# Setup tables as planned steps, PSUM banks from the plan, and a given order for each engine up to the third up step

## The chip, the core and the metric

The kernel runs on one core of a Trainium2 chip. The metric is the device time of one execution in microseconds (us). Five engines work side by side, each through its own instructions in order: TensorE (PE, with its weight loads as PEld), VectorE (DVE), ScalarE (ACT), GpSimd (POOL) and SyncE (SP). SP and POOL also issue the DMA transfers of this kernel; an engine that waits at one instruction holds up all that stands behind it on the same engine.

## What is computed

The reference is an RWKV-style linear attention followed by an MLP mixer. There are 4 batches, 8 heads, 768 tokens and 48 channels a head (8 x 48 = 384 = `d_model`).

```python
for t in range(S):                                    # attention, for every batch and head
    cur = einsum('bhd,bhe->bhde', u * k[t], v[t])
    y[t] = einsum('bhd,bhde->bhe', r[t], state + cur)
    state = w * state + einsum('bhd,bhe->bhde', k[t], v[t])
x = y as [batch, token, 384]
h = relu(x^T @ w_tok1) @ w_tok2                       # mixes tokens: 768 -> 256 -> 768
u = x + h^T
out = u + relu(u @ w_ch1) @ w_ch2                     # mixes channels: 384 -> 1536 -> 384
```

## The kernel before

**Tiling.** The sequence of a batch is cut into 6 chunks of 128 tokens; one chunk of one batch is a *unit*, 24 in all (unit u belongs to batch u // 6). For a unit, k and r are multiplied by tables of powers of w, so that the recurrence becomes matrix products: inside the chunk a masked 128 x 128 product for each head, across chunks a state S.

**The steps of a unit, by the names of the plan.** `kp` and `rp` multiply the loaded k and r by the tables `wn` and `wp` into the tile `kpr` (on DVE or POOL). `trk` and `trr` transpose the two halves of `kpr` on PE into `tr_ps`; `rkk`/`rkr` (or one `rk`) copy the result to SBUF on ACT. `at` makes the scores on PE (`at_ps0`, `at_ps1`), and `AT0`, `AT1` mask them on DVE; where a unit is listed in `raw`, ACT first copies the scores to bf16 and DVE masks the copy. `pr` and `pg` give the term with u, `vb` casts v on ACT, `yd` multiplies it in, `kv` and `S` make the next state, `yS` and `y` the output in PSUM, and `x` adds up the unit's result on DVE.

**The mixer of a batch.** `hid` (w_tok1, 2 matmuls for each of 6 units, tiles `wtok`, `h_ps`), `hr` (its relu into `h1r`), `bk`/`ub`/`ux` (w_tok2), `us` and `tu`/`uT` (sum and transpose), then 2 x 12 *up steps* `z` (w_ch1, 3 matmuls of 384 columns each, tile `z_ps`) with their relus `zr`, and the *down steps* `h` (w_ch2, also named `wch`) with `os` and the store. Up and down steps of a batch are interleaved on PE with the attention units of the next one.

**What sets the order.** Function `graph` lists all steps with their predecessors, the engines they can run on and a time for each; class `Plan` then runs a list scheduler over them (`run`): at each moment the step of lowest `rank` that is ready gets a free engine. The instructions are issued in the order of the planned start, engine by engine, so the plan fixes each engine's order for good; its times do not bind the chip. The plan also treats transfers as steps: loads are issued by SP (`i:k6`, `i:r6`, ...; k, r and v of 192 KB each a unit), the seven weight transfers by POOL (`i:w0` to `i:w6`: 0 is w_tok1, 1 is w_tok2, 2, 6 and 4 are parts of w_ch1, 3 and 5 the halves of w_ch2). In the plan a transfer is one step on one resource "DMA", which takes one transfer at a time.

**Lines that matter here.** Loads of units 0 to 5 are issued at once at the start, in the order of `FIRST`. The load of k of unit 6 is held back until unit 5's output is made, and all later loads stand behind it on SP:

```python
    hold={6: ('y', 5), 21: ('us', '2_2')},
    wafter={0: 'x:r4', 1: 'x:r4', 2: 'rp5', 6: 'rp5', 4: 'kp5', 3: 'rp5', 5: 'rp5'},
```

The tables are set up outside the plan's view: the step `lnw` takes two logarithms on ACT and then, in the same step, three products on DVE (`wr`, the tile `wp`); the plan knows only the ACT part. In the units 13 to 15 the step `vb` also issues one more exponential on ACT (`wp_as_read`, tiles `wp<-lnw`), which the plan does not count. Four PSUM banks form a ring (pool `psM`) for transposes, up and down steps and others, and the framework hands them out. All engine instructions go through one helper, so the profile gives them one line (L515, in the changed kernel L579), and tiles tell them apart.

Of the kernel before, what the change touches and what calls it, by code (L numbers as in the profile page):

```python
# [23 lines left out]
T = 128  # L24
# [11 lines left out]
class Step:  # L36
    def __init__(self, name, ways, after, take, give, rank, emit):
        self.name, self.ways, self.take, self.give, self.rank, self.emit = name, ways, take, give, rank, emit
        self.after = [a for a in after if a is not None]
        self.then, self.left, self.ready = [], len(self.after), 0.0  # L40
        self.engine = self.start = self.end = self.seen = self.sends = None
        for a in self.after:
            a.then.append(self)


class Plan:
# [3 lines left out]
    def __init__(self, banks, busy_until, in_flight, relax_from=0.0):  # L50
        self.relax_from = relax_from
        self.steps, self.banks, self.busy_until, self.in_flight, self.used = [], banks, busy_until, in_flight, []
# [20 lines left out]
    def run(self):  # L73
# [4 lines left out]
        todo, times = len(self.steps), [0.0]  # L78
        while todo:
# [4 lines left out]
            while again:  # L84
                again = False
                for s in sorted(open_, key=lambda s: (s.rank, s.ready)):
# [8 lines left out]
                    way = min(s.ways, key=lambda w: max(now, free.get(w[0], 0.0)) + w[2] + (w[4] if len(w) > 4 else 0.0))  # L95
                    eng, busy, seen = way[:3]
                    shares = len(way) > 3 and way[3]
                    if free.get(eng, 0.0) > now:
                        continue
                    if shares and port["DVE" if eng == "POOL" else "POOL"] > now:  # L100
                        heapq.heappush(times, max(port.values()))
                        continue
                    s.engine, s.start, s.end, s.seen = eng, now, now + busy, now + seen
                    free[eng] = s.end
# [5 lines left out]
                    if s.take:  # L110
                        i = banks.index(min(banks))
                        banks[i], held[s.name] = float("inf"), i
                        self.used.append([now, float("inf"), s.name])
# [16 lines left out]
    def fill(self, since, until, least, margin, each, emit):  # L130

        mine = sorted((s for s in self.steps if s.engine == "PE"), key=lambda s: s.start)
        for a, b in zip(mine, mine[1:]):
# [4 lines left out]
            taken = sum(1 for x in self.used if x[0] < b.start and x[1] > a.end)  # L138
            n = int((b.start - a.end - margin) / each)
            if b.start - a.end >= least and taken < self.banks and n > 0:  # L140
                s = self.add(f"fill{a.name}", [("PE", n * each, n * each)], emit=emit(n))
                s.engine, s.start, s.end, s.seen = "PE", a.end, a.end + n * each, a.end + n * each
# [3 lines left out]
def products_in_turn(steps, apart):  # L146


    both = [s for s in steps if s.engine in ("DVE", "POOL") and s.name.rstrip("0123456789") in ("kp", "rp", "ku", "rku", "yd", "wGm")]
    dve = [s for s in steps if s.engine == "DVE"]  # L150
    behind, d = {}, None
    for s in both:
        if s.engine == "DVE":
            d = s if len(s.after) and s.name[:2] != "yd" or s.ways[0][0] == "POOL" else d
        elif d is not None and s.start - d.end < apart:
# [13 lines left out]
def graph(do, cfg):  # L169

    p = Plan(4, cfg.get("busy_until", dict(ACT=3.9, DVE=3.6, POOL=5.0, PE=5.4)), cfg.get("in_flight", 8), cfg.get("relax_from", 0.0))
# [10 lines left out]
    lnw = p.add("lnw", [("ACT", 0.49, 0.6)], rank=-100, emit=do("lnw"))  # L182
    tables, wps = {}, {}
    tables[0] = setup = p.add("wn0", [("ACT", 0.52, 0.65)], [lnw], rank=-99, emit=do("wn", 0))
    wps[0] = p.add("wp0", [("ACT", 0.52, 0.65)], [lnw], rank=-98, emit=do("wp", 0))
    for g in (1, 2):
        tables[g] = p.add(f"wn{g}", [("ACT", 0.52, 0.65)], [lnw], rank=g - 0.6, emit=do("wn", g))
        wps[g] = p.add(f"wp{g}", [("ACT", 0.52, 0.65)], [lnw], rank=g - 0.5, emit=do("wp", g))

    wu = p.add("wu", [("PE", 0.4, 0.6)], rank=-1, emit=do("wu"))  # L190
    uw = p.add("uw", [("DVE", 0.65, 0.8)], [wu], rank=0.05, emit=do("uw"))
# [4 lines left out]
    for n, (kind, i) in enumerate(cfg["transfers"]):  # L196
# [3 lines left out]
        elif kind != "w":  # L200
            for nm in cfg.get("lorder", "krv") if kind == "u" else kind:
                s = p.add(f"i:{nm}{i}", [("SP", cfg.get("sp", 0.65), 0.65)], fetched[-1:], rank=-1000 + n, emit=do("load", nm, i))
                fetched.append(s)
                gates[nm, i] = s
                loads[nm, i] = p.transfer(f"x:{nm}{i}", s, cfg.get("xload", {}).get(i, 1.01), cfg.get("xload", {}).get(i, 1.01) + 1.09 + cfg.get("slack", {}).get(f"{nm}{i}", 0.0), 0.0)
# [13 lines left out]
    for u in range(NU):  # L219
# [22 lines left out]
        else:  # L242
            trk = p.add(f"trk{u}", [("PE", 0.235 * f, 0.235 * f + 0.2)], [kp], take=True, rank=r, emit=do("trk", u))
            trr = p.add(f"trr{u}", [("PE", 0.235 * f, 0.235 * f + 0.2)], [rp, trk], rank=r - 0.5, emit=do("trr", u))
            if u == 0:
                p.wait(wu, [trr])
# [22 lines left out]
        a0 = p.add(f"AT0_{u}", [("DVE", 0.597, 0.75)], [atq[0]], rank=r, emit=do("AT", u, 0))  # L269
        if u in cfg.get("raw", ()):  # L270
            raw = p.add(f"raw{u}", [("ACT", 0.5, 0.65)], [at], rank=r, emit=do("raw", u))
            a1 = p.add(f"AT1_{u}", [("DVE", 0.33, 0.48, True)], [raw], rank=r, emit=do("ATr", u))
            at_free = [a0, raw]
        else:
            a1 = p.add(f"AT1_{u}", [("DVE", 0.597, 0.75)], [atq[1]], rank=r, emit=do("AT", u, 1))
            at_free = [a0, a1]
# [139 lines left out]
CFG = dict(apart=2.0,   # L416
    transfers=[("u", u) for u in range(0, 6)]
# [20 lines left out]
    slack={'v5': 3.0},  # L438
# [5 lines left out]
    cold=(1.8, 1.8, 1.8, 1.3),  # L444
    xload={6: 0.33},
    wtime=(3.0, 2.6, 1.55, 5.2, 3.1, 3.9, 1.55),
    raw=(0, 1, 5, 8, 11),
# [13 lines left out]
    warm=(2, 4),  # L461
# [6 lines left out]
def kernel(  # L468
# [32 lines left out]
    psM = ctx.enter_context(tc.tile_pool(name="psM", bufs=4, space=bass.MemoryType.PSUM))  # L501
# [41 lines left out]
    idle_ps = psM.tile([128, 512], f32, name="idle_ps", tag="m")  # L543
    w_ps = psM.tile([128, dm + 2 * D], f32, name="w_ps", tag="m")
# [6 lines left out]
    pe.matmul(w_ps[:, 0:dm], ones, row, start=True, stop=True, skip_group_check=True)  # L551
# [66 lines left out]
    def lnw_(eng):  # L618
        act.activation(lnw, w_ps[:, 0:dm], Ln)
        act.activation(lnr.rearrange("p q d -> p (q d)"), w_ps[:, dm:], Ln)  # L620
        shape = [128, 2, R, D]
        for g in range(G):
            dve.tensor_mul(wr[:, g], lnr.unsqueeze(2).to_broadcast(shape), iota_r[:, g].unsqueeze(1).unsqueeze(3).to_broadcast(shape))
# [11 lines left out]
    def wu(eng):  # L635
        M0["wu"] = psM.tile([128, 2, HP], f32, name="wu_ps", tag="m")
# [9 lines left out]
    def ubc(eng):  # L646
# [14 lines left out]
             ("k", 4, 0), ("r", 4, 0), ("v", 4, 0), ("r", 4, 1), ("r", 5, 0), ("k", 5, 0), ("r", 5, 1), ("v", 5, 0))  # L661
# [83 lines left out]
    def tr(j, i):  # L745
        if j == 0:
            L[i]["tr"] = psM.tile([128, 2, HP, T], bf16, name="tr_ps", tag="m")
# [51 lines left out]
    def raw(eng, i):  # L799
        L[i]["raw"] = apool.tile([128, HP, T], bf16, name="raw", bufs=2)  # L800
        act.copy(L[i]["raw"], L[i]["at"][1])

    def ATr(eng, i):
        L[i]["AT"][1] = apool.tile([128, HP, T], bf16, name="AT1", bufs=LEAD)
        dve.tensor_mul(L[i]["AT"][1], L[i]["raw"], mask_b.unsqueeze(1).to_broadcast([128, HP, T]))
# [11 lines left out]
    def pg(eng, i):  # L817
        own = i in CFG.get("ydp", ())
        to = psM.tile([128, H], f32, name="g_ps", tag="m") if own else kvs[1][:, i % G]
# [74 lines left out]
    def hid(eng, b, c):  # L894
        if c == 0:
            M[b]["h1"] = [psM.tile([128, dm], f32, name="h1_ps", tag="m") for _ in range(2)]
# [16 lines left out]
    def bk(eng, b, c):  # L913
        M[b]["bk", c] = psM.tile([128, dm], f32, name="hT_ps", tag="m")
# [12 lines left out]
    def tu(eng, b, c):  # L927
        M[b]["t", c] = psM.tile([128, 3, 128], bf16, name="t_ps", tag="m")
# [10 lines left out]
    def ux(eng, b, sg, m):  # L939
        if m < 2:  # L940
            M[b]["ut", sg, m] = psA.tile([128, HP, T], f32, name=f"at_ps{m}", tag=f"at{m}").rearrange("p a t -> p (a t)")[:, 0:dm]
        else:
            M[b]["ut", sg, m] = psM.tile([128, dm], f32, name="ut_ps", tag="m")
# [18 lines left out]
    def z(eng, b, sg, j):  # L962
        if (b, sg) not in Z:
            Z[b, sg] = zpool.tile([128, NJ, dm], bf16, name="zr")
        M[b]["z", sg, j] = psM.tile([128, dm], f32, name="z_ps", tag="m")
# [7 lines left out]
    def h(eng, b, c, q, part, parts):  # L973
        sg, si = divmod(c, 3)
        cols = ts(part, dm // parts)
        if q == 0:
            M[b]["h", c, part] = psM.tile([128, dm // parts], f32, name="h2_ps", tag="m")
# [81 lines left out]
```

## Time and profile before

| what | value |
|---|---|
| runs | 165.55, 165.68, 166.1 us; median 165.68 us |
| profiled execution | span 164.0 us from the first to the last instruction |
| median of the runs less that span | 1.68 us |
| PE busy | 156.6 us (95% of the span), 1466 matmuls |
| DVE, ACT, POOL busy | 109.2, 88.5 and 67.1 us |
| chain that ended last | PE 85%, DVE 5%, ACT 5%, issue 2% |
| DMA | 26.26 MB, mean 160 GB/s |

A span row gives, for each engine, its busy time in a stretch and its number of instructions; a timeline row gives the start in us, the length, the engine, the operation and its tiles, and in brackets how long the engine had been idle and what ended it. "q0" is the queue of the transfers that POOL issues, "q1" that of SP's. The granted clock of PE stands at 1.00 in all rows.

### The profile page before, as it was taken

How to read it: one execution, taken by the hardware profiler on the slowest of the kernel's cores; microseconds unless marked ns; L12 is line 12 of the kernel's file. 1: busy time of each engine (PE TensorE's matmuls, PEld its weight loads, DVE VectorE, ACT ScalarE, POOL GpSimd, SP SyncE). 2: the span in 40 equal slices, each digit the busy share in tenths (PEclk: the TensorE clock that was granted, in tenths of full speed). 3: DMA queues.
4: the chain of work that ended last, by engine and by line, in shares of the span. 5: the costliest groups of instructions: out<-in, count | busy, mean ns of one | idle time of the engine just before them, and what ended most of it. 6: DMA issues, size and time to landing. Idle time of an engine off the chain costs nothing.

```text
span 164.0 us, 3852 instructions
## 1 busy us (share of the span) xinstructions
PE 156.6 (95%) x1466; PEld 100.9 (62%) x1466; DVE 109.2 (67%) x225; ACT 88.5 (54%) x194; POOL 67.1 (41%) x83
## 2 busy tenths in 40 slices
PE   6798999999999999899999999999999999999992
PEld 3277865566677666566566565666656655666562
DVE  6679897602289889899899899977876582012021
ACT  3898662595488466789706450077253502914900
POOL 8748893000037848566875856204750000000000
DMA  4999999999798997999999972999990028012012
GB/s 92 221 223 207 173 154 173 192 194 232 153 231 233 190 213 220 196 238 180 217 231 133 263 135 67 203 231 194 194 240 4 0 53 216 19 52 96 0 48 96
DMA packets 87307, 26.26 MB, mean 160 GB/s; under 512 B 76665, under 2 KB 87290, under 8 KB 87290
## 3 DMA queue, kind: packets, MB, share of 16 engines
q1 hardware_dynamic: 83392, 22.88, 65.1%
q0 software_dynamic: 3888, 3.15, 13.1%
q8 instruction: 11, 0.18, 0.4%
q14 instruction: 6, 0.05, 0.2%
q10 hardware_dynamic: 10, 0.00, 0.0%
HBM read 20.65 MB, written 4.72 MB: 155 GB/s over the span
## 4 chain that ended last, share of the span: by engine, by line
PE 85%; DVE 5%; ACT 5%; issue 2%; POOL 1%; DVEq 0%; ACTq 0%
PE h_ps L515 33%; PE z_ps L515 29%; PE y_ps L515 5%; PE at_ps L515 5%; PE tr_ps L515 4%; PE hT_ps L515 3%; PE kv_ps L515 3%; ACT rk L515 2%; DVE AT L515 2%; DVE x_b L515 1%; PE w_ps L515 1%; DVE yd L515 1%; POOL kpr L515 1%; ACT wp L515 1%; ACT raw L515 1%
## 5 line engine op out<-in xcount | busy, mean ns | idle before, releaser
L515 ACT ACTIVATE zr<-z_ps 128x384 bf16<-128x384 f32 x94 | 45.4, 492 | 44.2 <-PE z_ps L515 44.1
L515 PE MATMUL z_ps<-uT,wch 128*128 128x384 bf16 x288 | 52.5, 326 | 0.2
L515 PE MATMUL h_ps<-wch,zr 128*128 128x384 bf16 (+1 forms) x300 | 52.5, 320 | 0.0
L515 PEld LDWEIGHTS <-zr 128*128 128x128 bf16 x300 | 27.9, 98 | 15.5 <-issue 0.2
L515 PEld LDWEIGHTS <-wch 128*128 128x128 bf16 x288 | 26.7, 98 | 16.1 <-issue 0.4
L515 POOL TENSOR_TENSOR yd<-vb,adg 128x384 f32<-128x384 bf16 x18 | 15.5, 859 | 42.2 <-ACT adg L515 25.1
L515 DVE TENSOR_TENSOR AT<-at_ps,mask 128x512 bf16<-128x512 f32 x43 | 27.9, 683 | 0.6 <-PE at_ps L515 0.5
L515 DVE TENSOR_TENSOR osb<-u_sb,h_ps 128x384 f32<-128x384 bf16 (+1 forms) x22 | 11.7, 532 | 23.5 <-PE h_ps L515 23.4
L515 POOL TENSOR_TENSOR kpr<-ld_r,wp 128x384 bf16<-128x384 f32 x16 | 17.0, 1064 | 5.3 <-DVE yd L515 2.2
L515 ACT COPY rk<-tr_ps 128x512 bf16<-128x512 bf16 x28 | 15.5, 589 | 5.5 <-PE tr_ps L515 5.1
L515 PEld LDWEIGHTS <-kpr 128*128 128x128 bf16 x192 | 13.6, 108 | 6.1 <-POOL kpr L515 2.6
L515 DVE TENSOR_TENSOR x_b<-y_ps,yd 128x384 bf16<-128x384 f32 x24 | 13.3, 552 | 5.8 <-PE y_ps L515 5.5
L515 POOL TENSOR_TENSOR kpr<-ld_k,wn 128x384 bf16<-128x384 f32 x15 | 15.5, 1031 | 2.1 <-PE z_ps L515 1.1
L515 PEld LDWEIGHTS <-rk 48*128 48x128 bf16 (+1 forms) x272 | 11.1, 100 | 6.4 <-issue 2.8
L515 PE MATMUL tr_ps<-ident,kpr 128*128 128x128 bf16 x112 | 12.3, 247 | 2.0 <-ACT rk L515 1.0
L515 ACT CAST vb<-ld_v 128x384 bf16<-128x384 f32 x24 | 12.3, 511 | 3.5 <-DMA ld_v<-in_v_dram 3.5
L515 DVE TENSOR_TENSOR u_sb<-x_b,hT_ps 128x384 bf16<-128x384 bf16 x21 | 10.4, 546 | 1.1 <-PE hT_ps L515 1.1
L515 PEld LDWEIGHTS <-wtok 128*128 128x128 bf16 x90 | 8.0, 98 | 4.8 <-issue 0.6
L515 PEld LDWEIGHTS <-AT 128*128 128x128 bf16 x192 | 8.6, 99 | 3.6 <-DVE AT L515 0.7
L515 PE MATMUL at_ps<-rk 48*128 48x128 bf16 x192 | 10.4, 233 | 0.4 <-ACT rk L515 0.4
L515 DVE TENSOR_TENSOR kpr<-ld_k,wn 128x384 bf16<-128x384 f32 x9 | 5.9, 658 | 7.0 <-DMA ld_k<-in_k_dram 7.0
L515 PE MATMUL h_ps<-x_b,wtok 128*128 128x384 bf16 x48 | 10.2, 326 | 0.1
(91 smaller groups left out, 154.2 us busy)
## 6 DMA issues: line engine op xcount, KB each, us to landing
ld_k<-in_k_dram SPq DMA_DIRECT2D x24, 192.0 KB, 3.6
ld_v<-in_v_dram SPq DMA_DIRECT2D x24, 192.0 KB, 3.7
out_dram<-osb SPq DMA_DIRECT2D x23, 192.0 KB, 2.5
ld_r<-in_r_dram SPq DMA_DIRECT2D x28, 96.0 KB, 3.2
ld_r<-in_r_dram SPq DMA_DIRECT2D x10, 192.0 KB, 3.8
wch<-in_moe_w_ch_dram POOLq DMA_DIRECT2D x3, 576.0 KB, 12.6
wtok<-in_moe_w_tok_dram POOLq DMA_DIRECT2D x2, 384.0 KB, 5.1
wch<-in_moe_w_ch_dram POOLq DMA_DIRECT2D x2, 288.0 KB, 5.6
```

Source lines behind the costliest of these rows:

```text
L515: ins = tc.keep_in_program_order(f(*args, **kw))
```

## The change

**Setup as steps.** The logarithm of w is taken in two halves (`ln0`, `ln1`), the one for r in `lnr`; the three products `wr0` to `wr2` become steps that may run on DVE or POOL. The plan gets times at which the four small inputs of the setup are there.

**Banks.** `Plan.run` notes the ring bank that it gives each step, and the kernel asks for just that bank (pool `psM` with four tags and one buffer each).

**A given order.** `CFG["order"]` lists, for PE, ACT, DVE and POOL, every step up to the third up step in a fixed order (the step sits at the front of its engine's list or it waits). `lands` gives a landing time for each of the 18 first loads, `half_clock` a time until which PE's steps are counted 1.85 times as long (in place of `cold`, factors for the first units). The first loads change places: the second half of r of unit 4 goes ahead of v of unit 4. `raw` moves from units 0, 1 and 5 (one half each) to unit 4 (one half) and unit 5 (both). The dummy matmuls at the start go from 2 + 4 to 2 + 3. The rest of the steps is placed by the list scheduler as before, from the state in which the given order leaves it.

```diff
+                    if s.name in self.place:
+                        if front(self.place[s.name]) != s.name:
+                            continue
+                        ways = [w for w in s.ways if w[0] == self.place[s.name]]
+                    else:
+                        ways = [w for w in s.ways if w[0] not in self.order or front(w[0]) is None]
...
+                    if eng == "PE" and now < self.half_clock:
+                        busy, seen = busy * 1.85, busy * 1.85 + seen - busy
...
-    lnw = p.add("lnw", [("ACT", 0.49, 0.6)], rank=-100, emit=do("lnw"))
+    lns = [p.add(f"ln{h}", [("ACT", 0.23, 0.40)], [pre["w" + "AB"[h]]], rank=-100 + 0.1 * h, emit=do("ln", h)) for h in range(2)]
+        wrs[g] = p.add(f"wr{g}", [("DVE", 0.467, 0.62, True), ("POOL", 0.955, 1.06, True)], [lnr], rank=-98 if g == 0 else g - 0.9, emit=do("wr", g))
...
+                if (nm, i) in cfg.get("lands", {}):
+                    gates[nm, i] = s
+                    loads[nm, i] = p.add(f"x:{nm}{i}", [("-", 0.0, cfg["lands"][nm, i])], rank=-5000)
+                    continue
...
+        POOL=(
+            "kp1 kp2 wGm kp3 rp3 kp4 rp4 i:w0 rp5 i:w1 i:w2"
+        ).split(),
...
-    cold=(1.8, 1.8, 1.8, 1.3),
+    half_clock=19.0,
-    wtime=(3.0, 2.6, 1.55, 5.2, 3.1, 3.9, 1.55),
-    raw=(0, 1, 5, 8, 11),
+    wtime=(2.4, 1.95, 1.6, 5.2, 3.1, 3.9, 1.55),
+    raw=((4, 1), (5, 0), (5, 1), (8, 1), (11, 1)),
...
-    psM = ctx.enter_context(tc.tile_pool(name="psM", bufs=4, space=bass.MemoryType.PSUM))
+    psM = ctx.enter_context(tc.tile_pool(name="psM", bufs=1, space=bass.MemoryType.PSUM))
+    def bank(shape, dtype, name, which=None):
+        return psM.tile(shape, dtype, name=name, tag=f"m{now[-1].bank if which is None else which}")
...
-             ("k", 4, 0), ("r", 4, 0), ("v", 4, 0), ("r", 4, 1), ("r", 5, 0), ("k", 5, 0), ("r", 5, 1), ("v", 5, 0))
+             ("k", 4, 0), ("r", 4, 0), ("r", 4, 1), ("r", 5, 0), ("k", 5, 0), ("r", 5, 1), ("v", 4, 0), ("v", 5, 0))
```

**What it moves on POOL.** The place is the issue of the weights. In the kernel before, POOL's order around it reads (`kpr_130<-ld_r` is `rp` of unit 5, `wtok_160` w_tok2, `wch_161` w_ch1 and `wch_162` w_ch2):

```order
L515 DMA wtok_160<-in_moe_w_tok_dram 128x2x768
L515 TENSOR_TENSOR kpr_130<-ld_k,wn 128x8x48
L515 TENSOR_TENSOR kpr_130<-ld_r,wp 128x2x4x48
L515 DMA wch_161<-in_moe_w_ch_dram 128x3x384 x2
L515 DMA wch_161<-in_moe_w_ch_dram 128x3x768
L515 DMA wch_162<-in_moe_w_ch_dram 128x6x384 x2
L515 TENSOR_TENSOR yd<-vb,adg 128x384
```

The same place in the changed kernel, where `kpr_132<-ld_k` is `kp` of unit 6:

```order
L579 DMA wtok_159<-in_moe_w_tok_dram 128x6x256
L579 TENSOR_TENSOR kpr_130<-ld_r,wp 128x2x4x48
L579 DMA wtok_160<-in_moe_w_tok_dram 128x2x768
L579 DMA wch_161<-in_moe_w_ch_dram 128x3x384 x2
L579 DMA wch_161<-in_moe_w_ch_dram 128x3x768
L579 TENSOR_TENSOR kpr_132<-ld_k,wn 128x8x48
L579 DMA wch_162<-in_moe_w_ch_dram 128x6x384 x2
L579 TENSOR_TENSOR yd<-vb,adg 128x384
```

The `kp` of unit 6, on DVE before, now stands on POOL between the parts of w_ch1 and the two halves of w_ch2; `kp` of unit 5 went to DVE.

**What it moves on PE.** The place is the end of the third up step (`z_ps`, three matmuls). Before, the fourth up step follows at once, and unit 6's first transposes come some 75 matmuls later, between two down steps (`h_ps`). In the changed kernel:

```order
L579 MATMUL z_ps<-uT,wch_161 128x384
L579 LDWEIGHTS wch_161
L579 MATMUL z_ps<-uT,wch_161 128x384
L579 LDWEIGHTS kpr_132
L579 MATMUL tr_ps<-ident,kpr_132 128x128
L579 LDWEIGHTS kpr_132
L579 MATMUL tr_ps<-ident,kpr_132 128x128
L579 LDWEIGHTS kpr_132
L579 MATMUL tr_ps<-ident,kpr_132 128x128
L579 LDWEIGHTS kpr_132
L579 MATMUL tr_ps<-ident,kpr_132 128x128
L579 LDWEIGHTS wch_161
```

The four transposes of unit 6's k stand directly behind the third up step, ahead of the fourth.

**What it moves on ACT.** The place is the relu of the token mixer of batch 1 (`h1r<-h_ps`, two of 384 columns). Before:

```order
L515 COPY rk<-tr_ps 128x512 x2
L515 ACTIVATE h1r<-h_ps 128x384 x2
L515 COPY adg<-kv_ps 128x8
L515 ACTIVATE wp<-lnw,iota 128x384
L515 CAST vb<-ld_v 128x384
L515 COPY rk<-tr_ps 128x512 x2
```

In the changed kernel:

```order
L579 COPY rk<-tr_ps 128x512 x2
L579 COPY adg<-kv_ps 128x8
L579 ACTIVATE wp<-lnw,iota 128x384
L579 CAST vb<-ld_v 128x384
L579 ACTIVATE h1r<-h_ps 128x384 x2
L579 COPY rk<-tr_ps 128x512 x2
```

The exponential and the cast of unit 13 went ahead of the two relus, and on PE the `kv` matmuls of unit 13, which read that cast, went ahead of the `hT_ps` matmuls that read the relus.

158 lines of the change are left out of this document (102 added, 56 removed), and 3 rows, old and new, of the table PE.

## The prediction

> **What bounds the kernel now.** I first read the busy time by stretches; the columns are PE, PEld, DVE, ACT and POOL busy (instructions), granted clock, DMA share and GB/s.
>
> ```profile
> 10.00:19.00 9.00, 8.20 (x106) 6.89 (x102) 8.49 (x20) 7.49 (x19) 5.83 (x7) 1.00 0.91 201
> 19.00:24.20 5.20, 4.96 (x85) 3.43 (x81) 4.96 (x10) 3.09 (x8) 5.18 (x7) 1.00 1.26 168
> 30.10:67.00 36.90, 36.78 (x411) 24.73 (x409) 23.44 (x48) 24.78 (x56) 13.99 (x15) 1.00 0.99 207
> 67.00:73.30 6.30, 5.55 (x71) 3.91 (x69) 5.93 (x13) 5.00 (x13) 4.02 (x5) 1.00 1.05 220
> 73.30:136.00 62.70, 62.70 (x563) 38.99 (x563) 51.78 (x97) 27.99 (x61) 28.08 (x29) 1.00 0.80 158
> ```
>
> From 30.1 us on, PE is idle for 0.12 us in 36.9, then loses 0.75 us around 70, and nothing up to 136. So whatever moves the third up step moves the end by as much, in either direction, and any wait put into PE's order after 30 us is paid in full. Before 27 us the chain of waits runs over DVE instead:
>
> ```profile
> 19.80 1.27 DVE AT L515 x2
> ...
> 26.55 0.57 DVE x_b L515
> 27.16 0.48 PE h_ps L515 x2
> ...
> 31.82 0.17 PE t_ps L515 x3
> 31.99 0.65 PE z_ps L515 x4
> ```
>
> Unit 5's result (`x`) ends at 27.1; three matmuls of 0.163 us behind 31.99 end the third up step; ends of matmuls are modelled, and I count 32.4. Those 5.3 us hold the same mixer steps in both kernels, so the gain at the front is what `x` of unit 5 gains.
>
> **Part 1, the front.** These rows show its start, and the products and masks of the first 26 us on DVE by kind:
>
> ```profile
> 4.33 0.49 ACT L515 ACTIVATE lnw<-w_ps 128x384 f32<-128x384 f32 x1 [1.41 <-PE w_ps L515]
> 5.61 1.27 POOL L515 TENSOR_TENSOR kpr<-ld_k,wn 128x384 bf16<-128x384 f32 x1 [0.99 <-POOL bm L515]
> 10.29 0.42 DVE L515 TENSOR_TENSOR pr<-tr_ps,rk 128x512 bf16<-128x512 bf16 x1
> ...
> L515 DVE TENSOR_TENSOR AT<-at_ps,mask 128x512 bf16<-128x512 f32 x9 | 5.9, 683 | 0.0
> L515 DVE TENSOR_TENSOR x_b<-y_ps,yd 128x384 bf16<-128x384 f32 x6 | 3.3, 551 | 1.0 <-PE y_ps L515 0.7 <-DVE pr L515 0.2
> L515 DVE TENSOR_TENSOR yd<-vb,g_ps 128x384 f32<-128x384 bf16 x6 | 3.3, 545 | 0.0
> L515 DVE TENSOR_TENSOR wp<-lnr,iota_r 128x384 f32<-128x384 f32 x3 | 2.3, 821 | 1.3 <-ACT lnr L515 1.3
> L515 DVE TENSOR_TENSOR kpr<-ld_k,wn 128x384 bf16<-128x384 f32 x1 | 0.5, 548 | 0.0
> ```
>
> The logarithm waited for all of `w_ps`; in halves I let it start some 0.7 us earlier, which puts the first k product at 4.9 on DVE (0.55) in place of 5.61 on POOL (1.27). From there DVE has 42 instructions up to `x` of unit 5, against 33 from 10.29 before: the same 9 full masks, 3 short ones, 6 `pr`, 6 `yd`, 6 `x`, but five k and r products instead of one, the three table products and the small ones for u. With the durations above (0.42 for `pr` and the short mask, 0.55 for `yd` and the tables when POOL is quiet) they add up to 22.3 us against 18.1. Before, 18.1 took 27.1 - 10.3 = 16.8 us, since one instruction starts before the last has ended; in that ratio 22.3 take 20.7, to 25.6, a gain of 1.5. With no wait left (two masks of 0.683 in 1.27 overlap by about 0.08 each) they take 18.9, to 23.8, a gain of 3.3. Some of the waits do go: POOL's `rp` of unit 4 waited for its load until 18.37, and its second half is now issued one place earlier. I take **-1.8**, nearer the ratio, and keep -0.8 to -2.8. The third up step then ends at 32.4 - 1.8 = 30.6. The banks of the ring cost nothing here: PE's 0.12 us idle up to 67 leaves no wait for a bank to remove.
>
> **Part 2, unit 6 behind the third up step.** PE's next instructions now are four transposes that read the k product of unit 6, on POOL, which waits for its load, which SP holds until unit 5's `y`. Before:
>
> ```profile
> 18.37 0.99 POOL L515 TENSOR_TENSOR kpr<-ld_r,wp 128x384 bf16<-128x384 f32 x1 [0.48 <-DMA ld_r<-in_r_dram]
> 20.12 1.02 POOL L515 TENSOR_TENSOR kpr<-ld_k,wn 128x384 bf16<-128x384 f32 x1
> 22.03 4.02 POOL L515 DMA_DIRECT2D wch<-in_moe_w_ch_dram x5
> 26.42 0.37 SPq L515 DMA_DIRECT2D ld_k<-in_k_dram  x1
> 37.50 0.56 DVE L515 TENSOR_TENSOR kpr<-ld_k,wn 128x384 bf16<-128x384 f32 x1 [5.11 <-DMA ld_k<-in_k_dram]
> 43.54 0.61 PE L515 MATMUL tr_ps<-ident,kpr 128*128 128x128 bf16 x8
> ```
>
> Issued at 26.42, that load was used at 37.50, 11.1 us later, and nobody noticed, since its transposes stood at 43.5. It was slow because the weights were on the way. What each queue moved (packets, MB, share) from 0 to 30.0 us for POOL's, then from 26.4 to 30.0, then from 30.0 to 35.5:
>
> ```profile
> q0 software_dynamic: 2170, 1.76, 42.6%
> ...
> q0 software_dynamic: 671, 0.69, 117.8%
> ...
> q0 software_dynamic: 998, 0.85, 94.8%
> q1 hardware_dynamic: 918, 0.18, 28.8%
> ```
>
> No byte of SP's queue moved in the first 3.6 us, then 0.033 MB/us beside 0.155 of the weights. In the changed kernel the load is issued 1.8 earlier, at 24.6. Ahead of it on POOL's queue stand w_tok1, w_tok2 and w_ch1, 1,920 KB or 1.97 MB, but not w_ch2. By 30.0 POOL's queue had moved 1.76 MB of these before; the first three now start some 0.3 to 0.8 us later and w_ch1 1 us earlier, so I leave its end at about 30.8. The load moves nothing until 28.2, 2.6 x 0.033 = 0.09 MB until 30.8, and the other 0.11 MB at some 0.2 MB/us until 31.4; with the 0.4 to 1 us that a landing takes beyond that, it is there at **32.0**. The product on POOL (1.02) ends at 33.0, the transposes start at 33.05, and PE has stood since 30.6: **+2.5**. Behind the transposes wait all up steps, and behind them ACT's and DVE's relus.
>
> For the bounds and the next part, the median times to landing and the first down step:
>
> ```profile
> ld_k<-in_k_dram SPq DMA_DIRECT2D x24, 192.0 KB, 3.6
> wtok<-in_moe_w_tok_dram POOLq DMA_DIRECT2D x2, 384.0 KB, 5.1
> 38.65 0.33 PE L515 MATMUL h_ps<-wch,zr 128*128 128x384 bf16 x1
> ```
>
> The median landing of a k load is 3.6 us, which gives 28.2 and a product at 29.2, no stall; the 11.1 us of before give 35.7 and transposes at 36.7, a stall of 6.1.
>
> **Part 3, w_ch2.** Its halves were the last two of the five issued from 22.03, at about 24.4 and 25.2; now they stand on POOL behind the product, at 33.0 and 33.8. A transfer of 384 KB landed in 5.1; 576 KB need 1 us more, 39.1, and 40 to 41 beside SP's loads. PE reaches its first down step 14 up steps of 0.49 behind the transposes (33.3), at 40.1; before it was at 38.65. The second half is needed 3.4 us after the first and takes 3 to 4 more. Between 0 and 2.0; I take **+0.4**.
>
> **Part 4, ACT in the mixer of batch 1.**
>
> ```profile
> 65.94 0.50 PE L515 MATMUL h_ps<-x_b,wtok 128*128 128x384 bf16 x2
> 66.31 0.87 ACT L515 ACTIVATE h1r<-h_ps 128x384 bf16<-128x384 f32 x2 [1.20 <-PE h_ps L515]
> 67.31 1.29 PE L515 MATMUL hT_ps<-h1r,wtok 128*128 128x384 bf16 x6
> 67.75 0.62 ACT L515 ACTIVATE wp<-lnw,iota 128x384 f32<-128x384 f32 x1
> 68.27 0.50 ACT L515 CAST vb<-ld_v 128x384 bf16<-128x384 f32 x1
> 68.82 0.33 PE L515 MATMUL kv_ps<-vb,kpr 128*128 128x96 bf16 x4 [0.22 <-ACT vb L515]
> 69.79 0.40 PE L515 MATMUL at_ps<-rk 48*128 48x128 bf16 x8 [0.45 <-ACT rk L515]
> ```
>
> The relus ended 1.2 us behind the last `h_ps`, hidden by down steps and transposes; the exponential and the cast came after, beside the six `hT_ps` matmuls. Now those two (0.52 + 0.40 = 0.92 from start to start) come first, `kv` waits for them, and `hT_ps` for the relus behind them. 0.92, plus some 0.65 of the relus uncovered since a down step no longer stands there, less the 0.67 that PE waited here before: **+0.9**; 0 if the last unit's scores hold PE longer, 2.0 if the transposes behind it wait too.
>
> **Sum.** 164.0 - 1.8 + 2.5 + 0.4 + 0.9 = 166.0 us for the span. The runs' median lies 1.68 above the profiled span (165.68), so **167.7 us**.
>
> **The rule that speaks against Part 2.** The Trainium skill ("DMA: Bandwidth & Descriptors", Queues, rings and completion order) says that each DMA engine goes round-robin between the queues for which it has work. By that, unit 6's load would move from the start, which the first 3.6 us of the row above contradict. It is the second rival.
>
> **The rivals.** (a) *The load is as quick as a lone one*, 3.6 us: no stall, w_ch2 in time, 164.0 - 1.8 + 0.9 = 163.1, so 164.8, faster. It decides where the load lands before 29.5. Only the dip of DMA traffic around 24 to 25 us before speaks for it, and w_ch1 now is issued into that dip. (b) *The load shares from about 1 us after its issue*: 0.033 x 5.2 = 0.17 MB by 30.8, landed at 31.0 at the latest, perhaps 30.6; product at 31.6, stall 1.1, w_ch2 +0.2: 164.4, so 166.1, no difference. For it: the shares from 30.0 to 35.5. Against: no packet of SP's before 30.0. (c) *The load takes as long as before*, in 11.1 us: 164.0 - 1.8 + 6.1 + 1.0 + 0.9 = 170.2, so 171.9. Against it: w_ch2, which it ran beside, is not there now. The Trainium skill ("TensorE: Matmul & The Clock Gate", What's actually happening) has PE drop to half its clock after an idle window of about 3.4 us; by that (c) would cost some 1.7 us more, an estimate from that window. No wait here is as long as that window, but the same four transposes do run at two speeds:
>
> ```profile
> 17.83 0.63 PE L515 MATMUL tr_ps<-ident,kpr 128*128 128x128 bf16 x4
> 19.79 0.38 PE L515 MATMUL tr_ps<-ident,kpr 128*128 128x128 bf16 x4
> ```
>
>  (d) *The front gains nothing*: then load and up step shift alike, and with Parts 2 to 4 it ends at 169.5, inside the forecast's own case.
>
> **How the numbers follow.** Forecast, a stall of 1.5 to 4.5 us, 0.58, with its own range from 166.3 to 169.8; (a) 0.12; (b) 0.15; (c) 0.15. About 0.3%, or 0.5 us, is what a measurement of this kernel tells from no change. Faster: (a) and a little of (b), 0.14. Same: most of (b), 0.12. Slower: the rest, 0.74. The range reaches into (a) on one side and (c) on the other: 164.6 to 170.6.
>
> **What would show it.** Part 1: `x` of unit 5 at about 25.3, DVE without waits over 0.5 us before it. Part 2: PE idle for 2 to 3 us behind the third up step, ended by POOL's `kpr<-ld_k`, and POOL idle until its load at about 32. Part 3: a down step that waits for a transfer near 40. Part 4: `kv_ps<-vb` and `hT_ps` waiting for ACT around 69 to 72. The prediction is wrong if the load of unit 6 lands before 30 or PE has no wait over 1 us there.

## The result, and the profile after

The changed kernel took 172.95 us (median; 172.6 to 173.47), the kernel before 165.67 on the same chip: a ratio of 1.0446, interval 1.0418 to 1.0475. The forecast was 167.7 with a range to 170.6: slower was right, the size was far off. A run more than 1.5% above the fastest of its kernel is left out of the medians and ratios given here; only h2_tiles and h_three_tiles have such runs. The profiled execution is the slowest of the four (173.47): its span is 171.8 us, 7.8 above the 164.0 of before, where the sum had +2.0. Its stretches, with the columns of the prediction's first view:

```profile
19.00:24.20 5.20, 4.10 (x71) 2.96 (x70) 5.03 (x12) 4.09 (x10) 3.59 (x5) 1.00 0.73 88
30.10:67.00 36.90, 31.65 (x311) 19.95 (x309) 16.09 (x35) 20.42 (x44) 12.24 (x13) 0.95 0.92 184
67.00:73.30 6.30, 6.03 (x91) 4.07 (x90) 6.05 (x14) 3.31 (x7) 3.78 (x4) 1.00 0.99 216
73.30:136.00 62.70, 61.65 (x584) 38.52 (x583) 52.47 (x99) 33.25 (x73) 29.80 (x32) 1.00 0.83 168
```

PE, which lost 0.12 us between 30.1 and 67, now stands for 5.25 us there, and its mean clock falls to 0.95. PE's timeline says where:

```profile
30.67 0.65 PE L579 MATMUL z_ps<-uT,wch 128*128 128x384 bf16 x3
35.48 0.61 PE L579 MATMUL tr_ps<-ident,kpr 128*128 128x128 bf16 x4 [4.16 <-POOL kpr L579]
35.88 8.42 PE L579 MATMUL z_ps<-uT,wch 128*128 128x384 bf16 x42
44.70 0.34 PE L579 MATMUL h_ps<-wch,zr 128*128 128x384 bf16 x1 [0.40 <-DMA wch<-in_moe_w_ch_dram]
...
48.98 1.30 PE L579 MATMUL h_ps<-wch,zr 128*128 128x384 bf16 x7 [0.69 <-DMA wch<-in_moe_w_ch_dram]
```

The third up step ends at 31.3 (32.5 before, both modelled: a gain of 1.15). Then come the transposes of unit 6, 4.16 us late, and further on two waits for w_ch2. POOL's timeline shows the cause of both:

```profile
20.61 0.99 POOL L579 TENSOR_TENSOR kpr<-ld_r,wp 128x384 bf16<-128x384 f32 x1 [2.97 <-PE at_ps L579]
21.55 0.78 POOL L579 DMA_DIRECT2D wtok<-in_moe_w_tok_dram  x1
22.33 2.29 POOL L579 DMA_DIRECT2D wch<-in_moe_w_ch_dram  x3
34.44 0.98 POOL L579 TENSOR_TENSOR kpr<-ld_k,wn 128x384 bf16<-128x384 f32 x1 [9.82 <-DMA ld_k<-in_k_dram]
35.38 1.71 POOL L579 DMA_DIRECT2D wch<-in_moe_w_ch_dram  x2
```

POOL waited for the load of unit 6 until 34.44, not 32.0, and w_ch2 went out behind that. What the two DMA queues moved in the first 4.3 us behind the issue of that load at 25.7 (packets, MB, share):

```profile
q0 software_dynamic: 969, 0.83, 121.5%
q1 hardware_dynamic: 61, 0.01, 2.5%
```

POOL's queue had nearly all of it. The page's row of the 576 KB pieces, from issue to landing, gives their median, which is the value of the last piece of w_ch1, issued at 23.85 as the third from 22.33: it landed at 33.7.

```profile
wch<-in_moe_w_ch_dram POOLq DMA_DIRECT2D x3, 576.0 KB, 9.9
```

The page's chain of waits puts 12% of the span on DMA; before, no DMA stood in it:

```profile
PE 70%; DMA 12%; ACT 9%; issue 3%; DVE 2%; POOL 2%; POOLq 0%
```

The 42 up matmuls from 35.88 take 8.42 us. The stretch in which they and the transposes start has half the clock:

```profile
35.48:38.60 3.12, 3.12 (x13) 1.73 (x14) 1.30 (x3) 1.57 (x3) 1.61 (x2) 0.50 1.03 184
```

Measured from the start of one matmul to the start of the next, what is lost behind the third up step beyond the kernel before is about 4.3 us at the transposes, 0.2 in them (four take 0.40 where they take 0.22 at full clock), 1.4 in the nine up matmuls behind them (0.320 instead of 0.162 each), 1.4 at the two halves of w_ch2, 1.3 in and just ahead of the mixer of batch 1 (2.7 of waits against 1.4) and 0.3 at one up step near 102: 8.9 us, less the front's 1.15, for 7.8. The half clock is 1.6 of it.

### The profile page after: what moved, and what is told of

Same layout as the page of the kernel before. It is cut to its first block, busy times and chain, and to the rows that moved or that the text cites. A ratio compares the mean times of both kernels' runs of the same rounds, so it can differ in the third digit from the quotient of the medians.

```text
span 171.8 us, 3823 instructions
## 1 busy us (share of the span) xinstructions
PE 157.3 (92%) x1460; PEld 100.3 (58%) x1460; DVE 108.9 (63%) x229; ACT 90.4 (53%) x197; POOL 61.6 (36%) x78
## 4 chain that ended last, share of the span: by engine, by line
PE 70%; DMA 12%; ACT 9%; issue 3%; DVE 2%; POOL 2%; POOLq 0%
PE h_ps L579 30%; PE z_ps L579 22%; DMA wch<-in_moe_w_ch_dram 7%; DMA ld_k<-in_k_dram 5%; PE y_ps L579 4%; PE at_ps L579 4%; PE tr_ps L579 3%; PE hT_ps L579 3%; PE kv_ps L579 2%; ACT rk L579 2%; ACT wp L579 1%; ACT vb L579 1%; POOL kpr L579 1%; PE w_ps L579 1%; ACT uT L579 1%
## 5 line engine op out<-in xcount | busy, mean ns | idle before, releaser
L579 ACT ACTIVATE zr<-z_ps 128x384 bf16<-128x384 f32 x95 | 46.0, 492 | 40.1 <-PE z_ps L579 39.8
L579 PE MATMUL z_ps<-uT,wch 128*128 128x384 bf16 x288 | 53.5, 332 | 0.1
L579 PEld LDWEIGHTS <-wch 128*128 128x128 bf16 x288 | 27.3, 99 | 17.2 <-issue 1.9
L579 POOL TENSOR_TENSOR yd<-vb,adg 128x384 f32<-128x384 bf16 x18 | 15.4, 854 | 42.5 <-ACT rk L579 16.2
L579 POOL TENSOR_TENSOR kpr<-ld_k,wn 128x384 bf16<-128x384 f32 x12 | 12.4, 1037 | 14.5 <-DMA ld_k<-in_k_dram 9.8
L579 DVE TENSOR_TENSOR pr<-tr_ps,rk 128x512 bf16<-128x512 bf16 x14 | 5.9, 420 | 16.0 <-ACT rk L579 15.8
L579 POOL TENSOR_TENSOR kpr<-ld_r,wp 128x384 bf16<-128x384 f32 x13 | 13.7, 1050 | 4.7 <-PE at_ps L579 3.0
```

What stands on the lines that cost most here:

```text
L579: ins = tc.keep_in_program_order(f(*args, **kw))
```

## Is it one wait or two? Moving each, and both

Theory 1: the transposes' wait and w_ch2's wait cover each other, so that neither alone is worth much. Theory 2: the wait behind the third up step is the loss. Three kernels, each with one list of moves in the order of issue. All steps and banks stay; only the place of these steps changes.

```diff
 a_w2_first   POOL:  ... i:w2 i:w6 i:w4 i:w3 i:w5 kp6      (was: i:w4 kp6 i:w3 i:w5)
 b_trk_late   PE:    ... h0_0_0 h0_0_1 trk6                (was: z0_0_0 trk6 z0_0_3)
              ACT:   rkk6 behind zr0_1_4
 c_both       both
```

**w_ch2 ahead of unit 6's product.**

> The changed kernel with one move in POOL's order: both halves of w_ch2 are issued ahead of unit 6's k product instead of behind it. PE's order is untouched. Theory 1 (the load of unit 6 gets through only when POOL's stream of weights is through, so the product and w_ch2 stand in each other's way): with w_ch2 in the stream the load takes the 11.1 us of the kernel before, 25.7 + 11.1 = 36.8, the transposes start near 37.9 instead of 35.5 and PE stands 6.6 us instead of 4.2; the waits of 1.4 us for w_ch2 go. 172.95 + 2.4 - 1.4 = 173.9, between 173 and 175. Theory 2 (the load takes 8.7 us whatever stands behind it): only the 1.4 us go, 171.5.

Measured 175.47 us, 1.0611 [1.0562, 1.066]. PE's timeline behind the third up step, and POOL's product:

```profile
38.14 0.61 PE L584 MATMUL tr_ps<-ident,kpr 128*128 128x128 bf16 x4 [6.85 <-POOL kpr L584]
```

```profile
37.10 0.99 POOL L584 TENSOR_TENSOR kpr<-ld_k,wn 128x384 bf16<-128x384 f32 x1 [10.86 <-DMA ld_k<-in_k_dram]
```

The load took 11.4 us from its issue (25.7), the 11.1 of the kernel before and not the 8.7 of the changed one. So the time of this load is set by what POOL has in its queue, and the move that spares w_ch2 its wait makes the other longer. Theory 2's 171.5 falls. The median is 0.5 us above the range of theory 1, the profiled run (174.54) inside it.

**The transposes behind the up steps.**

> The changed kernel with one move on PE and ACT: the four transposes of unit 6's k and their copy stand 14 up steps and two pieces of a down step later. POOL's order is untouched. Theory 1: PE no longer stands at 31.3 and reaches the first down step near 38.2, but w_ch2 is still issued behind the product, at 35.4, and lands at 44.7 and 48.9 as before; the stall moves there, with its half clock, and nearly nothing is gained: 172 to 173.5. Theory 2 (PE's wait behind the third up step is the loss, w_ch2 a matter of 1.4 us): 4.3 us of wait, 0.6 us of slow transposes and 1.4 us of slow up steps go, 166.7.

Measured 173.79 us, 1.0493 [1.0455, 1.0531]: nothing gained, a little more lost, and 0.3 above the range of theory 1. PE's timeline, POOL's issue of w_ch2, and the stretch behind the wait:

```profile
33.71 5.54 PE L584 MATMUL z_ps<-uT,wch 128*128 128x384 bf16 x33 [0.87 <-DMA wch<-in_moe_w_ch_dram]
43.44 0.50 PE L584 MATMUL h_ps<-wch,zr 128*128 128x384 bf16 x1 [4.20 <-DMA wch<-in_moe_w_ch_dram]
```

```profile
35.29 1.71 POOL L584 DMA_DIRECT2D wch<-in_moe_w_ch_dram  x2
```

```profile
43.40:47.00 3.60, 3.56 (x18) 2.25 (x19) 0.00 (x0) 0.58 (x1) 0.00 (x0) 0.50 1.25 225
```

The wait of 4.2 us went to the first down step, with half the clock behind it. The wait at 33.71 is new: the seventh up step now comes early enough to wait for the last piece of w_ch1, which in the changed kernel lay hidden under the 4.16 us.

**Both.**

> Both moves together: w_ch2 ahead of unit 6's k product on POOL, and the transposes behind the up steps. Theory 1: neither wait is left, 172.95 - 4.3 - 0.6 - 1.4 - 1.4 = 165.2, between 164.8 and 166.2, so about the kernel before: the front's gain of 1.15 us less what the mixer of batch 1 loses. Theory 3 (the order of everything behind the front is worse, not these two places): over 169.

Measured 167.48 us, 1.0134 [1.01, 1.0168]. The two moves alone bring +2.5 and +0.8 us; together they bring -5.5. That is theory 1, and theory 3 (over 169) falls. It is 1.3 above the range I gave, though. PE's timeline, and POOL's product:

```profile
33.76 5.54 PE L585 MATMUL z_ps<-uT,wch 128*128 128x384 bf16 x33 [0.91 <-DMA wch<-in_moe_w_ch_dram]
```

```profile
37.23 0.99 POOL L585 TENSOR_TENSOR kpr<-ld_k,wn 128x384 bf16<-128x384 f32 x1 [10.99 <-DMA ld_k<-in_k_dram]
```

The wait for w_ch1 is there again, and the product's lateness (37.23) hurts nobody now. I had left that wait out, and set the batch-1 mixer too low.

## The half clock by itself

The same late transposes as in a_w2_first, with idle matmuls in the wait:

```diff
+            if i == 6:
+                t = bank([128, 512], f32, "fill_ps")
+                for _ in range(29):
+                    pe.matmul(t, idle[:, 0:128], idle, start=True, stop=True)
             L[i]["tr"] = bank([128, 2, HP, T], bf16, "tr_ps")
```

> The changed kernel with w_ch2 ahead of unit 6's product on POOL (run a_w2_first, 175.47 us, where PE stood for 6.85 us ahead of the transposes), and 29 idle matmuls of 512 columns (about 0.216 us each, 6.3 us) put ahead of those transposes, so that PE is busy through most of the wait. No result of the kernel depends on them. If the half clock after the wait costs time of its own (0.16 us more for each of nine matmuls in the changed kernel, and some 0.6 us at the transposes): about 2 us less, 173.5. If the slow matmuls there have another cause, or the dummies only push the transposes back: 175.5 or more.

Measured 173.33 us, 1.0481 [1.0451, 1.051]: 2.1 less than a_w2_first by the medians, 1.3 by the spans of the profiled executions (172.8 and 171.5). PE's timeline:

```profile
31.15 6.42 PE L584 MATMUL fill_ps<-idle 128*128 128x512 bf16 x28
38.24 0.40 PE L584 MATMUL tr_ps<-ident,kpr 128*128 128x128 bf16 x4 [0.67 <-POOL kpr L584]
38.48 6.99 PE L584 MATMUL z_ps<-uT,wch 128*128 128x384 bf16 x42
```

The transposes start 0.1 us later than in a_w2_first and still end earlier (0.40 instead of 0.61), and the 42 up matmuls take 6.99 us instead of 8.26 there (8.42 in the changed kernel). So the slow matmuls come from PE's idleness before them, and cost 1.3 us of their own between the two profiles, 2.1 between the medians. The runs of a_w2_first lie 1.8 us apart (174.54 to 176.37), those of this kernel 0.33 (173.21 to 173.54). The mean granted clock fits that: 0.98 in three runs of a_w2_first and 0.969 in its slowest, 1.00 in all four here. Only one run of each was traced.

## The load issued earlier

```diff
-            first = INS["".join(map(str, CFG["hold"][i]))]
+            first = INS["y3" if i == 6 else "".join(map(str, CFG["hold"][i]))]
```

> The changed kernel, but the load of unit 6's k (and with it all later loads of SP) is held for the output of unit 3 instead of unit 5, so it is issued near 21.4 us, ahead of w_tok2, w_ch1 and w_ch2, instead of at 25.7. Orders are untouched. Theory 1 (the load gets through between POOL's transfers, in the order of their issue, and then the product, w_ch2 and the transposes are in time): it lands near 25 to 27, no stall behind the third up step, w_ch2 issued by 28; w_ch1 lands up to 1 us later and the up steps wait for that: 166.5 to 169. Theory 2 (it lands 8.7 us after its issue, or only when POOL's stream has run dry near 33): it lands at 30 or later, w_ch2 goes out at 31 or later and down steps wait: 169 to 173.

Measured 168.48 us, 1.0195 [1.0159, 1.023], as theory 1 had it. The timelines of SP's queue, of POOL and of PE:

```profile
21.44 0.37 SPq L579 DMA_DIRECT2D ld_k<-in_k_dram  x1
```

```profile
24.70 1.02 POOL L579 TENSOR_TENSOR kpr<-ld_k,wn 128x384 bf16<-128x384 f32 x1
```

```profile
31.92 0.39 PE L579 MATMUL tr_ps<-ident,kpr 128*128 128x128 bf16 x4
32.55 1.64 PE L579 MATMUL z_ps<-uT,wch 128*128 128x384 bf16 x9 [0.24 <-DMA wch<-in_moe_w_ch_dram]
35.87 5.54 PE L579 MATMUL z_ps<-uT,wch 128*128 128x384 bf16 x33 [1.69 <-DMA wch<-in_moe_w_ch_dram]
```

Issued 4.3 us earlier, 0.1 ahead of w_tok2, the load was there after 3.3 us at most, and the transposes did not wait. PE now waits 1.9 us for w_ch1; that the loads behind this one on SP, issued earlier too, take their share from it is likely and was not tested. The order of every engine is the changed kernel's; only the hold differs, and 4.5 of the 7.3 us are back. So most of what the order loses, it loses only with a load that comes as late as this one did.

## What is left: ACT's exponentials and the weights

**The exponentials out of `vb`**, on top of both moves:

```diff
     def vb(eng, i):
-        if i + 1 not in split and len(natural) < G:
-            wp_as_read((i + 1) % G)
...
+            if s.name in EXPS:          # EXPS = {"vb11": 2, "raw1_11": 0, "rk13": 1}
+                wp_as_read(EXPS[s.name])
```

> Both moves, and the three exponentials that ride in the step vb of units 13, 14 and 15 are issued by ACT one or two steps earlier, behind vb of unit 11, the raw copy of unit 11 and rk of unit 13, where the profile of the changed kernel shows ACT idle for 0.67, 0.70 and 1.17 us. If they are what the mixer of batch 1 loses (kv of unit 13 waits 0.54, kv of unit 15 0.35, and half of the 1.2 us of small waits at hT_ps and t_ps between 74.7 and 80): 1.0 to 1.5 us below the kernel with both moves. If the waits only pass to the relus or to rk: within 0.4 of it.

Measured 166.73 us, 1.0085 [1.0063, 1.0107]: 0.75 below c_both, between the two expectations and nearer the first. In the changed kernel ACT's timeline and the wait on PE's were

```profile
73.54 0.62 ACT L579 ACTIVATE wp<-lnw,iota 128x384 f32<-128x384 f32 x1
74.06 0.50 ACT L579 CAST vb<-ld_v 128x384 bf16<-128x384 f32 x1
74.46 0.87 ACT L579 ACTIVATE h1r<-h_ps 128x384 bf16<-128x384 f32 x2
```

```profile
74.61 0.33 PE L579 MATMUL kv_ps<-vb,kpr 128*128 128x96 bf16 x4 [0.38 <-ACT vb L579]
```

With the exponential elsewhere the waits of units 13 and 15 at `kv` are gone (0.54 and 0.35 from start to start), while the small ones at `hT_ps` and `t_ps` stayed (0.23, 0.22, 0.29 and 0.27, in c_both as in f_both_exps) and a new one of 0.30 came at `t_ps`. They have another cause, which the runs don't settle. So have two waits just ahead of the mixer, 0.6 us together, which end with DVE (a mask and an `osb`); they are in the changed kernel, in c_both and in f_both_exps alike.

**The weights earlier on POOL.** A first form of this (g_weights_early, 165.53 us, and h_three_tiles, 164.94) put `rp` of unit 5 behind the issues in the program as well, so that unit 5's transposes read the tile before it was written: these two kernels leave that wait out, and their times are not compared with the rest.

> The kernel f_both_exps (166.73 us) with one more move on POOL: rp of unit 5, which POOL waits 2.97 us for, stands behind w_tok2 and all of w_ch1 instead of ahead of them. Those are then issued from 17.6 instead of 21.55; POOL's four issues take 3.1 us, so rp of unit 5 itself still starts near 20.7. Theory: with both moves the seventh up step waits 0.9 to 1.1 us for the last part of w_ch1, which lands at 33.7 (32.86 in the kernel before), so part of the front's gain was given back to the weights; this wait goes: 165.6. Rival: the weights now take DMA time from the last first loads (v of units 4 and 5 land at 20.7) and the front ends later: 166.7 or more.

> The kernel g_weights_early, and the broadcast of w stands in three PSUM tiles, one for each half and one for the rows of r, instead of one. The two logarithm halves started at 4.29 in the changed kernel, behind all six matmul passes into that tile, and at 4.33 before, so the halves gained 0.04 us where I had counted on 0.7. If the one tile is the reason: the first half starts near 3.1 to 3.9, the first k product at 4.9 to 5.1 instead of 5.52, and up to 0.5 us of that reach the third up step: 0.3 to 0.5 below g_weights_early. If the logarithm waits for something else, or the front is bound by loads: the same time as g_weights_early.

The form that keeps all waits, on top of f_both_exps:

```diff
 POOL:  rp4 i:w0 i:w1 i:w2 i:w6 i:w4 rp5 i:w3 i:w5 kp6     (was: rp4 i:w0 rp5 i:w1 i:w2 i:w6 i:w4 i:w3 i:w5 kp6)
```

> The kernel f_both_exps (166.73 us) with the four issues of w_tok2 and w_ch1 on POOL put ahead of rp of unit 5, in the place of the 2.97 us that POOL waits for it. (In the runs g_weights_early and h_three_tiles that product was written behind unit 5's transposes in the program, so these read an old tile and did not wait for it; here it keeps its place.) They are issued from 17.6 instead of 21.55. Theory: with both moves the seventh up step waits 0.9 to 1.1 us for the last part of w_ch1, which lands at 33.7 (32.86 in the kernel before), so part of the front's gain was given back to the weights; this wait goes: 165.5. Rival: the weights take DMA time from the last first loads, or rp of unit 5 starts later than 20.7, and the front ends later by as much: 166.5 or more.

Measured 165.73 us, 1.0024 [1.0011, 1.0037], 1.0 below f_both_exps, as the theory had it. POOL's timeline, and PE's from the third up step on:

```profile
16.81 1.62 POOL L588 DMA_DIRECT2D wtok<-in_moe_w_tok_dram  x2
18.41 2.27 POOL L588 DMA_DIRECT2D wch<-in_moe_w_ch_dram  x3
20.81 0.99 POOL L588 TENSOR_TENSOR kpr<-ld_r,wp 128x384 bf16<-128x384 f32 x1
```

```profile
30.86 5.45 PE L588 MATMUL z_ps<-uT,wch 128*128 128x384 bf16 x32
```

No up step waits any more, and `rp` of unit 5 starts 0.2 later than it did. With four repairs the changed kernel is where it began, 0.24% above the kernel before.

**The logarithm's tile**, on top of g2_weights:

```diff
-    w_ps = bank([128, dm + 2 * D], f32, "w_ps", 1)
+    w_ps = [bank([128, dm // 2], f32, "w_ps", 1), bank([128, dm // 2], f32, "w_ps", 2), bank([128, 2 * D], f32, "w_ps", 3)]
...
```

> The kernel g2_weights with the broadcast of w in three PSUM tiles, one for each half and one for the rows of r, instead of one. The two logarithm halves started at 4.29 in the changed kernel, behind all six matmul passes into that tile (4.33 before), so the halves gained 0.04 us where I had counted on 0.7. If the one tile is the reason: the first half starts near 3.3, the first k product at 4.9 instead of 5.52, and the 0.6 us reach the third up step and the end: 0.4 to 0.6 below g2_weights. If the front is bound by its loads from 8 us on: the time of g2_weights.

Measured 166.11 us, 1.0047 [1.0023, 1.0071], over nine runs from 165.48 to 167.02; three more took 168.9 to 169.5, for which no trace is kept. It is not the gain expected. ACT's first row in the changed kernel, the same here, the stretches of three microseconds here, and those of g2_weights:

```profile
4.29 0.55 ACT L579 ACTIVATE lnw<-w_ps 128x192 f32<-128x192 f32 x2 [1.35 <-PE w_ps L579]
```

```profile
3.27 0.33 ACT L588 ACTIVATE lnw<-w_ps 128x192 f32<-128x192 f32 x1 [0.34 <-PE w_ps L588]
```

```profile
19.00:22.00 3.00, 1.63 (x28) 1.23 (x28) 2.84 (x7) 1.22 (x3) 2.99 (x5) 1.00 1.19 156
22.00:25.00 3.00, 2.50 (x39) 1.74 (x37) 2.31 (x6) 2.80 (x7) 1.27 (x2) 0.72 1.19 186
25.00:28.00 3.00, 3.00 (x28) 2.03 (x27) 1.60 (x5) 0.27 (x1) 0.00 (x0) 0.71 1.27 210
```

```profile
19.00:22.00 3.00, 2.66 (x47) 2.06 (x46) 2.84 (x6) 2.21 (x5) 2.87 (x5) 1.00 1.25 172
22.00:25.00 3.00, 2.65 (x47) 1.78 (x46) 2.99 (x7) 2.66 (x7) 1.47 (x2) 1.00 1.21 197
```

The first half did start 1.0 us earlier, so the one tile was the reason. PE then ran ahead of `rp` of unit 5, which stands on POOL behind the weights and starts at 20.60 here and at 20.81 there. The transposes of that tile, here and then in g2_weights:

```profile
21.68 0.40 PE L588 MATMUL tr_ps<-ident,kpr 128*128 128x128 bf16 x4 [0.86 <-POOL kpr L588]
```

```profile
21.85 0.40 PE L588 MATMUL tr_ps<-ident,kpr 128*128 128x128 bf16 x4 [0.23 <-POOL kpr L588]
```

So 0.2 us of the lead was left there. PE was busy 1.63 us of three, and its clock fell behind that: the third up step ends 0.8 later than in g2_weights instead of 0.6 earlier. The expectation had named the loads as the bound; in this profile it was POOL, and then the clock. The four fastest runs, with a mean clock of 1.00, took 165.48 to 165.71, so without the lost clock too most of the expected gain is missing.

**The same two findings on the kernel before.**

```diff
 k_before_exps    EXPS = {"rk11": 2, "rk12": 0, "rk13": 1}
 k2_before_tiles  as k_before_exps, and
+    wq_ps = psM.tile([128, 2 * D], f32, name="wq_ps", tag="m")       # the rows of r, out of w_ps
```

> The kernel before, with the exponentials of units 13, 14 and 15 taken out of vb and issued behind rk of units 11, 12 and 13, where its profile shows ACT idle for 0.76, 1.20 and 0.76 us. Between 67 and 73 us PE loses 0.38 at kv of unit 13, 0.6 at the scores behind rk and 0.24 at a transpose. If the exponential in front of vb causes the first two: 0.6 to 1.0 us faster than before. If kv and the scores wait for something else then (relus, DVE's u_sb): within 0.3 of before.

> k_before_exps, and the rows of r of the broadcast of w in a PSUM tile of their own, so that the logarithm of w does not wait for the two matmul passes of those rows (4.33 us before). If one tile is what it waits for: it starts near 3.9, and 0.4 us of the front go; the end follows if w_ch1 (landed at 32.86, first used by the seventh up step near 33.8) does not bind: 0.2 to 0.4 below k_before_exps. If the front's DVE chain has slack there: the same time as k_before_exps.

Measured 165.11 us, 0.9973 [0.996, 0.9986], and 164.63 us, 0.9955 [0.9936, 0.9974]. The first gained 0.4, less than the 0.6 to 1.0 expected; the wait of unit 13 at `kv` is gone, the one at its scores (0.24 instead of 0.45) only shorter, as PE's timeline of k_before_exps shows:

```profile
68.31 0.33 PE L518 MATMUL kv_ps<-vb,kpr 128*128 128x96 bf16 x4
...
69.18 0.40 PE L518 MATMUL at_ps<-rk 48*128 48x128 bf16 x8 [0.24 <-ACT rk L518]
```

In the second the logarithm starts where expected (ACT's timeline below), and 0.5 us follow at the end by the medians, though the runs of the two overlap (164.07 to 165.5 and 164.41 to 165.22). This version, without any of the change, is the fastest of those that keep all waits: 0.45% below the kernel before and 8.3 us below the changed one.

```profile
3.91 0.49 ACT L518 ACTIVATE lnw<-w_ps 128x384 f32<-128x384 f32 x1 [0.96 <-PE w_ps L518]
```

## Why the prediction was wrong

**Right:** the sign, the three places behind the front, and what each waits for: the stall by POOL's product for its load, the down steps by w_ch2, `kv` of unit 13 by ACT's exponential and cast. Rivals (a) and (b), quick loads, fell: SP's queue moved 0.01 MB beside 0.83 MB of POOL's in the first 4.3 us. That is not what the Trainium skill ("DMA: Bandwidth & Descriptors", Queues, rings and completion order) leads one to expect, by which each DMA engine goes round between the queues with work. Why SP's queue got so little is not shown here.

**The front, -1.8 in the sum, measured -1.15.** The step that failed is "in halves I let it start some 0.7 us earlier". Both halves started at 4.29 (4.33 before) and the first k product on DVE at 5.52, not 4.9 (DVE's timeline, with `x` of unit 5):

```profile
5.52 0.56 DVE L579 TENSOR_TENSOR kpr<-ld_k,wn 128x384 bf16<-128x384 f32 x1 [1.87 <-ACT wn L579]
...
25.91 0.56 DVE L579 TENSOR_TENSOR x_b<-y_ps,yd 128x384 bf16<-128x384 f32 x1
```

From there the count held: 22.3 us of instructions in the ratio of before was to take 20.7 us, and it took 20.9 (5.52 to 26.46). Run h2_tiles shows the reason for the late start: one PSUM tile, so one wait for all matmuls into it. So `x` of unit 5 ended at 26.46, not at 25.3, and gained 0.65 us. The other 0.5 us of the 1.15 was luck: it came between `x` and the third up step, which I had taken as the same in both kernels (before, PE lost 0.4 us at the transposes ahead of the second up step, and that went).

**The stall, +2.5 in the sum, measured +4.3: the first large error.** The step is "the first three now start some 0.3 to 0.8 us later and w_ch1 1 us earlier, so I leave its end at about 30.8". w_tok2 started 2.2 us later (21.55 against 19.32) and w_ch1 0.3 later (22.33 against 22.03), because `rp` of unit 5, which the rows on POOL's order show ahead of both, waited 2.97 us there. I had moved these issues along with the front without asking what they stand behind on their engine. By 30.0 POOL's queue had moved 1.59 MB, where I had started from the 1.76 MB of before. And the end of w_ch1 could have been read instead of added up from bytes: the page of before has its pieces of 576 KB from issue to landing,

```profile
wch<-in_moe_w_ch_dram POOLq DMA_DIRECT2D x3, 576.0 KB, 12.6
```

the median of w_ch1's last piece and the two halves of w_ch2. The piece of w_ch1 among them landed at 32.9 in that profile (33.7 now), 9.3 us after its issue. In the kernel before, the queue had moved as many bytes by 31.2, and the last piece of w_ch1 landed 1.7 later: a stream that shares the DMA engines with what is issued behind it does not end where its own bytes add up. The mechanism was right: the load comes through when POOL's stream lets it, by 34.4 here, by 37.1 with w_ch2 in the stream (a_w2_first), after 3.3 us ahead of the stream (e_hold_y3).

**The half clock, 0 in the sum, measured +1.6: the second.** It stood in the text only beside rival (c), as "some 1.7 us more", which is the right size. The forecast's own stall of 2.5 us was below the window of about 3.4 us that the Trainium skill ("TensorE: Matmul & The Clock Gate", What's actually happening) gives for an idle array; the stall that came, 4.16 us, was above. For whole waits the trace agrees with that rule: 0.50 of the clock for 3.1 us behind 4.16 us of waiting, 0.50 behind the 4.20 us of b_trk_late, full clock behind waits of 0.9 us (c_both) and 1.7 us (e_hold_y3). A sum whose stall may pass such a bound has a step in it, and the range should have carried it: 4.3 was inside the interval I gave the forecast (1.5 to 4.5), the 1.6 that it drags along were not. The range also ended at 170.6, below the 171.9 of my own rival (c).

**w_ch2, +0.4, measured 1.4.** Within its bounds (0 to 2.0); the issue was at 35.38 and 36.3, not 33.0 and 33.8, and since the up steps behind the stall were as late, only the difference counts. That the two waits hide each other was not in the prediction at all: it added them, and it is what a_w2_first, b_trk_late and c_both show (+2.5, +0.8, -5.5).

**The mixer of batch 1, +0.9, measured 1.3.** Inside 0 to 2.0, and right in cause for `kv`, as f_both_exps shows (0.75 comes back). But 0.6 of the waits end with DVE just ahead of the mixer, which the prediction did not have.

Together: 0.65 too much gain, 1.8, 1.6, 1.0 and 0.4 too little loss, and the 0.3 near 102 us: 5.75 of the 5.8 us between the forecast's span and the profiled one.

## What to carry to other kernels

An engine that issues transfers delays them by whatever waits ahead of them in its order; before a load is moved earlier in a sum, read what its queue still has to move, and take the landings from the page's issue rows. When two waits are found, undo both: here each move alone made the kernel slower, and both together gave 5.5 us back. A wait put into a saturated TensorE costs more than its length once it is long enough to lose the clock (1.6 us on top of 4.3 here, nothing on top of 0.9 or 1.7), so a stall's price has a step in it; idle matmuls in the wait bought that part back in d_dummies.

## What was not expected of the hardware

In h2_tiles no single wait of PE between 15 and 28 us is longer than 0.86 us, yet its clock fell to 0.72 and 0.71 of full between 22 and 28 us, behind three microseconds in which it was busy for 1.63. Busy for 2.66 of the same three (g2_weights) it kept the clock at 1.00. A sparse stretch can cost the clock like a whole wait; where the bound lies between these two, the runs don't say. And the length of the slow stretch is not fixed: in the changed kernel the matmuls are at full speed 3.3 us behind the wait, in b_trk_late, after a wait of the same length, only 5.9 us behind it, though PE was busy throughout (its stretch from 47 to 50 us below). Read in slices of one microsecond, the half clock lasts from 35.4 to 38.8 in the changed kernel and from 23.3 to 26.8 in h2_tiles, 3.4 us each, but from 34.3 to 41.1 in a_w2_first and from 42.5 to 49.4 in b_trk_late, 6.8 us each. So in these four traces it comes in pieces of 3.4 us, one or two of them, and the first begins before the wait has ended (0.9 us before in b_trk_late, 3.9 before in a_w2_first).

```profile
47.00:50.00 3.00, 3.00 (x15) 1.68 (x14) 0.00 (x0) 0.00 (x0) 0.00 (x0) 0.61 0.55 127
```
